# A state-space scan with a gated feed-forward block: running sums of logarithms as three bfloat16 parts, weight sums on the Vector engine in the second block, and a new order of lead-in and decays

## The chip, the cores and the metric

The kernel runs on one core of one Trainium2 chip. A core has five engines with instruction queues of their own: TensorE (PE, with its weight loads shown apart as PEld), VectorE (DVE), ScalarE (ACT), GpSimd (POOL) and SyncE (SP, which here only issues DMAs). Each queue runs in order, and engines wait for one another at semaphores. The metric is the time of one execution on the device in microseconds, as the median of several runs; less is better.

## What is computed

The reference is a chunked state-space scan (4 batches, 8 heads, 768 steps, head size 32, state size 16), followed by a normalised feed-forward block with gate (3072 tokens, 256 model columns, 1536 hidden columns). Cut to what matters:

```python
log_a = np.log(np.clip(a, 1e-6, 1.0))
for c in range(nc):                          # chunks of the sequence
    cum = np.cumsum(la, axis=-1)             # running sum of logs in the chunk
    L = np.exp(cum[..., :, None] - cum[..., None, :]) * causal
    M = np.einsum('bhin,bhjn->bhij', Cc, Bc) * L
    y[:, :, sl] = einsum(M, xc) + einsum(Cc, state) * np.exp(cum)[..., None]
    state = np.exp(la.sum(-1)) * state + einsum(Bc, xc, np.exp(cum[..., -1:] - cum))
x = y as (3072, 256)
xn = x / sqrt(mean(x * x) + 1e-6) * rms_g
g = xn @ w_gate
out = (g * sigmoid(g) * (xn @ w_val)) @ w_out
```

The three weight matrices come in as 64-bit floats, and the kernel turns them into fp32 itself.

## The kernel before

**Tiling.** The kernel uses chunks of 128 steps. Two neighbouring chunks are a pair p; two pairs (512 tokens) are a block, so there are 6 blocks and 12 pairs. The scan of block n+1 is woven into the gate products of block n. Block 0 has nothing ahead of it: its scan is the lead-in.

**Decay products.** For each pair and each half (four heads), the tile L needs the exponential of a difference of running sums, with the causal mask. `masked()` writes a large negative number above the diagonal into two PSUM banks with bfloat16 matmuls (L297). `sums()` adds the running sum of one index (L311, 128 columns each) and takes away that of the other (L316, 512 columns), as fp32 matmuls that select a row with `sel`. `decay()` is the exp on ACT (L323). The rows come from `sums_of_logs(k)`: two matmuls (L272) of the logs `la` with the running-sum matrix `mid` and its negative `nmid`, copied out by DVE and ACT (L275). That serves pairs 0 to 3. For later pairs `spread()` reads the rows back from a DRAM copy `rowd`, one row broadcast to all partitions, and `decays()` subtracts on DVE (L336), takes the exp on ACT (L339) and masks on POOL (L340).

**Rest of the scan.** `pad` and `turn` bring B and C into transposed form T (L347, L368, L370). `products` multiplies them (L391) and `decayed` applies L on DVE (L399). `scale` forms the decayed B and C (L356), `states` the states (L422 to L439), `outputs` the result y (L457, L466), which ACT evacuates as squares and as a copy (L482, L484). `norm_sums` and `norm_apply` give the normalised block xn (L494 to L513).

**Weights.** `fetch` loads a piece of a matrix, `begin` (a "b" in the plans, L156 to L165) and `finish` (an "f", L171 and L173) convert it on DVE and ACT. The plans say which step goes where, by hand.

**Gates and projection.** Block 0 uses plain products (`gate_val`, L530: tile f, 128 hidden columns; L538 is its silu, L543 the product h). Blocks 1 to 5 use a seven-product scheme for 2x2 blocks (`gates_and_values`, L582, with copies p at L587, sums c at L592, silu at L597, h at L601). It needs sums of weights, `combine_w` (L560), four operations for each of six column pairs, made on POOL during the projection of block 0, and sums of xn, `combine_x` (L567). `project` is the second product (L641), `put` copies it to `ob` on ACT (L646) and sends it out.

**What sets the order.** Nothing is scheduled by a planner: the program's text is the order on each engine. PSUM tiles rotate: `pair_of_banks` has three slots of two banks (slots 0 and 1 in a pool `first` that is closed before block 1, slot 2 in a pool that stays), `bank` two single ones. A matmul that opens a slot waits until what stood there has been read. ACT holds one function table at a time, exp or silu; `preload_act_table` loads one by hand.

Of the kernel before, what the change touches and what calls it, by code (L numbers as in the profile page):

```python
# [9 lines left out]
FP32 = mybir.dt.float32  # L10
# [9 lines left out]
def kernel(  # L20
# [208 lines left out]
    sel = const.tile([P, BH], FP32, name="sel")  # L229
    nc.vector.reduce_sum(out=sel, in_=ident.rearrange("p (c k) -> p k c", k=BH), axis=AX.X)  # L230
# [3 lines left out]
    nmid = const.tile([P, P], FP32, name="nmid")  # L234
    nc.vector.tensor_scalar(out=nmid, in0=mid, scalar1=-1.0, scalar2=None, op0=ALU.mult)
# [27 lines left out]
    nc.vector.tensor_scalar(out=la, in0=aT, scalar1=1e-6, scalar2=1.0,  # L263
                            op0=ALU.max, op1=ALU.min)
    nc.scalar.activation(out=la, in_=la, func=AF.Ln)

    rows, nrows = [], []

    def sums_of_logs(k):
        for rhs, rs, copy in ((mid, rows, nc.vector.tensor_copy), (nmid, nrows, nc.scalar.copy)):  # L270
            r_ps = bank("r_ps", (P, P))
            nc.tensor.matmul(out=r_ps, lhsT=laf[:, 2 * k * BH:(2 * k + 4) * BH], rhs=rhs,  # L272
                             start=True, stop=True)
            rs.append(const.tile([P, P], FP32, name="rows%d" % len(rows + nrows)))
            copy(out=rs[k], in_=r_ps)  # L275
# [25 lines left out]
    def sums(todo):  # L301

        work = []
        for p, half, e in todo:
            for i in range(2):
                b, c = divmod(2 * p + i, NC)
                k, q = (0, c) if c < 4 else (1, c - 2)
                work.append((slice(32 * q, 32 * q + 32), k, b * NH + 4 * half, e[:, i]))
        for o in range(4):
            for r, k, h, e in work:  # L310
                nc.tensor.matmul(out=e[:, o * P:(o + 1) * P],  # L311
                                 lhsT=sel[r, h + o:h + o + 1].to_broadcast([32, P]),
                                 rhs=rows[k][r], start=False, stop=False,
                                 tile_position=(r.start, 0), skip_group_check=True)
        for r, k, h, e in work:
            nc.tensor.matmul(out=e, lhsT=nrows[k][r],  # L316
                             rhs=sel[r, h:h + 4].unsqueeze(2).to_broadcast([32, 4, P]),
                             start=False, stop=True, tile_position=(r.start, 0),
                             skip_group_check=True)
# [234 lines left out]
    def combine_w(j, eng):  # L554
# [3 lines left out]
        for k, in0, in1, op in ((0, a21, a22, ALU.add), (1, s[:, :, 0], a11, ALU.subtract),  # L558
                                (2, a11, a21, ALU.subtract), (3, a12, s[:, :, 1], ALU.subtract)):
            eng.tensor_tensor(out=s[:, :, k], in0=in0, in1=in1, op=op)  # L560
# [8 lines left out]
    def gates_and_values(blk, todo):  # L569
# [36 lines left out]
        for j in range(last + 1):  # L606
# [37 lines left out]
    def put(blk, k, o):  # L644
        ob = ffn.tile([P, DM], FP32, tag="ob", name="ob")
# [16 lines left out]
    sums([(0, 0, ex), (1, 0, ey)])  # L662
    decay(0, 0, ex)
    decay(1, 0, ey)
    pad(0, nc.vector)
    turn(0, 0, nc.vector.tensor_copy, 3)
    turn(0, 1, nc.vector.tensor_copy, 3)
    ez = masked()
    sums([(0, 1, ez)])
    to_i, from_j = exp_of_sums()  # L670
    products(0, 0)
    decay(0, 1, ez)
    scale(0)

# [3 lines left out]
    full = const.tile([P, NC, BH], FP32, name="full")  # L678
    nc.scalar.activation(out=full, in_=full_ps, func=AF.Exp)
    pad(1, nc.gpsimd)  # L680
    turn(1, 0, nc.scalar.copy, 3)
    turn(1, 1, nc.scalar.copy, 3)
    products(0, 1)
    ew = masked()
    sums([(1, 1, ew)])
    turn_last(0, nc.scalar.copy)
    decay(1, 1, ew)
    fsel = const.tile([P, NC * NB, NH], FP32, name="fsel")
    nc.vector.tensor_tensor(
# [5 lines left out]
    products(1, 0)  # L695
    scale(1)
    outputs(0)
    products(1, 1)
    turn_last(1, nc.scalar.copy)
    states(1)  # L700
    sums_of_logs(1)
    outputs(1)
    convert("bb")
    norm_sums(0, range(NT))
    ex, ey, ez = masked(), pair_of_banks("e"), pair_of_banks("e")
    g0, g1, ew = [pair_of_banks(n) for n in ("gate", "gate", "e")]
    sums([(2, 0, ex)])
    decay(2, 0, ex)
    finish()
    finish()  # L710
    norm_apply(0, range(NT))
    products_gv(0, 0, g0)
    convert("bb")
    mask(ey)
    sums([(3, 0, ey)])
    decay(3, 0, ey)
    convert("ff")
    mask(ez)
    sums([(2, 1, ez)])
    convert("b")  # L720
    decay(2, 1, ez)
    convert("b")
# [3 lines left out]
    mask(ew)  # L726
    sums([(3, 1, ew)])
    decay(3, 1, ew)
    nc.scalar.preload_act_table(AF.Silu)
# [36 lines left out]
    todo[0] = []  # L766
    plan = ["ff", "bbf", "f", "bbf", "f", "bbf", "f", "bbf", "f", "b", "bf", ""]
    for f in range(NF):
        uv = gate_val(0, f, (g0, g1)[f] if f < 2 else None)
        convert(plan[f])  # L770
        hidden(0, f, *uv)
        if f == 3:
# [6 lines left out]
            rowd = dram.tile([NC * BH, P], FP32, name="rowd")  # L779
            nc.sync.dma_start(out=rowd[0:P], in_=rows[0])  # L780
            nc.sync.dma_start(out=rowd[P:NC * BH], in_=rows[1][2 * BH:4 * BH])
            rowv = rowd.rearrange("r m -> (r m)")
        run(todo[f])
    load_block(2)
    o = pair_of_banks("o").rearrange("p k (j m) -> p k j m", j=2)
# [76 lines left out]
```

## Time and profile before

| | us |
|---|---|
| median of 3 runs | 476.56 |
| lowest, highest | 476.41, 481.7 |
| the profiled execution | 481.5 |
| its span | 479.8 |

The span is the time from the first to the last instruction in the trace; the execution's own time is 1.7 us longer. In the profile a line such as "L641 PE MATMUL o<-wo,h ... x576 | 130.7, 386 | 4.5 <-DVE wo L173 4.5" is a group of instructions of one line and shape: how many, their busy time in us, the mean length of one in ns, then how long the engine stood idle right before them and who released it. An fp32 matmul has two records. The lengths of matmuls overlap, so the distance from one start to the next says what a matmul costs. The granted clock is that of PE: 1.00 is full speed, 0.50 is half.

### The profile page before, as it was taken

The numbers are of one execution on the slowest core, as the hardware profiler recorded it, in microseconds if no ns is written. First come the engines' busy times: TensorE is split into PE (matmuls) and PEld (weight loads), VectorE is DVE, ScalarE is ACT, GpSimd is POOL, SyncE is SP. The second block draws the span as 40 slices with busy tenths as digits, with TensorE's granted clock in tenths as the row PEclk, the third lists the DMA queues.
The fourth block names the chain that finished last, engine by engine and source line by source line (L and its number), as shares of the span: only waits on it lengthen the run. The fifth ranks groups of instructions, "written<-read, shape, count | busy, mean of one in ns | idle before, by whom it ended". The sixth has DMA issues, their size and how long they took to land.

```text
span 479.8 us, 7020 instructions
## 1 busy us (share of the span) xinstructions
PE 452.9 (94%) x2780; PEld 348.4 (73%) x2780; DVE 258.1 (54%) x486; ACT 200.3 (42%) x374; POOL 65.1 (14%) x94
## 2 busy tenths in 40 slices
PE   8989799996969999989999989999989999999997
PEld 4654344465858778878888878778878778888886
DVE  3556589759926574247555246555337551255510
ACT  3435644441545543344553254453264440145500
POOL 2020000028680000220000310001210000000000
PEclk9978899999779999999999999999999999999999
DMA  9980244582056200046200064300000000000000
GB/s 135 206 196 3 87 131 133 113 156 92 2 91 129 84 6 1 22 70 128 89 2 11 23 75 112 87 2 12 22 12 1 1 1 11 23 11 2 0 15 30
DMA packets 86656, 27.91 MB, mean 58 GB/s; under 512 B 76160, under 2 KB 80448, under 8 KB 86624
## 3 DMA queue, kind: packets, MB, share of 16 engines
q1 hardware_dynamic: 82464, 27.21, 25.0%
q10 hardware_dynamic: 4160, 0.26, 0.6%
q8 instruction: 22, 0.36, 0.3%
q14 instruction: 10, 0.08, 0.1%
HBM read 24.22 MB, written 3.24 MB: 57 GB/s over the span
## 4 chain that ended last, share of the span: by engine, by line
PE 86%; DVE 6%; ACT 4%; issue 3%; DMA 0%; POOL 0%; SPq 0%; ACTq 0%
PE gate L582 23%; PE o L641 20%; PE val L582 16%; PE gate L530 10%; PE g L391 3%; PE y L466 3%; PE tp L368 2%; PE e L311 2%; PE y L457 2%; PE e L316 1%; DVE L L336 1%; ACT p L587 1%; PE ms L494 1%; PE e L297 1%; ACT L L339 1%
## 5 line engine op out<-in xcount | busy, mean ns | idle before, releaser
L641 PE MATMUL o<-wo,h 128*128 128x256 f32 x576 | 130.7, 386 | 4.5 <-DVE wo L173 4.5
L641 PEld LDWEIGHTS o<-wo,h 128*128 128x128 f32 x576 | 110.5, 194 | 20.8 <-DVE wo L173 5.3
L592 DVE TENSOR_TENSOR c<-val,p 128x512 f32<-128x512 f32 x90 | 61.5, 691 | 84.5 <-PE val L582 54.4
L587 ACT COPY p<-gate 128x512 f32<-128x512 f32 x90 | 53.0, 589 | 48.9 <-PE gate L582 48.9
L582 PE MATMUL gate<-tx,sw 128*128 128x256 f32 x240 | 64.4, 391 | 4.9 <-ACT p L587 4.9
L582 PEld LDWEIGHTS gate<-tx,sw 128*128 128x128 f32 x240 | 43.3, 192 | 14.6 <-ACT p L587 6.3
L530 PE MATMUL gate<-xn,wgv 128*128 128x512 f32 x96 | 48.0, 646 | 4.1 <-DVE h L543 3.2
L597 ACT ACTIVATE c<-c 128x256 f32<-128x256 f32 x90 | 37.8, 420 | 32.2 <-DVE c L592 32.2
L601 DVE TENSOR_TENSOR h<-c 128x256 f32<-128x256 f32 x90 | 37.7, 419 | 13.7 <-ACT c L597 13.7
L646 ACT COPY ob<-o 128x256 f32<-128x256 f32 x24 | 8.8, 372 | 86.4 <-PE o L641 60.2
L483 POOL TENSOR_TENSOR sq<-sq 128x256 f32<-128x256 f32 x12 | 8.8, 736 | 238.5 <-ACT sq L482 238.5
L530 PEld LDWEIGHTS gate<-xn,wgv 128*128 128x128 f32 x96 | 18.7, 204 | 26.8 <-issue 20.2
L582 PE MATMUL gate<-xn,wgv 128*128 128x256 f32 x120 | 31.8, 389 | 4.0 <-ACT ob L646 4.0
L582 PE MATMUL gate<-tx,wgv 128*128 128x256 f32 x120 | 31.3, 383 | 3.4 <-ACT p L587 3.4
L582 PE MATMUL val<-xn,wgv 128*128 128x256 f32 x120 | 31.7, 387 | 0.0
L582 PE MATMUL val<-tx,sw 128*128 128x256 f32 x120 | 30.9, 380 | 0.0
L582 PE MATMUL val<-xn,sw 128*128 128x256 f32 x120 | 30.8, 379 | 0.0
L340 POOL TENSOR_SCALAR_AFFINE_SELECT L<-L 128x1024 f32<-128x1024 f32 x16 | 19.4, 1210 | 77.0 <-ACT L L339 77.0
L513 DVE SCALAR_TENSOR_TENSOR xn<-yt,gcol,rb 128x512 f32<-128x512 f32 x12 | 8.4, 746 | 39.6 <-PE rb L507 39.5
L582 PEld LDWEIGHTS gate<-xn,wgv 128*128 128x128 f32 x120 | 23.2, 194 | 7.6 <-ACT ob L646 4.4
L582 PEld LDWEIGHTS gate<-tx,wgv 128*128 128x128 f32 x120 | 22.4, 190 | 8.2 <-ACT p L587 5.4
L399 DVE TENSOR_TENSOR L<-g,L 128x1024 f32<-128x1024 f32 x16 | 19.6, 1223 | 13.0 <-PE g L391 12.4
(121 smaller groups left out, 542.1 us busy)
## 6 DMA issues: line engine op xcount, KB each, us to landing
L<-rowd SPq DMA_DIRECT2D x16, 512.0 KB, 5.6
xr<-in_x_dram SPq DMA_DIRECT2D x24, 128.0 KB, 3.6
wr<-in_moe_w_out_dram SPq DMA_DIRECT2D x6, 512.0 KB, 3.5
out_dram<-ob SPq DMA_DIRECT2D x24, 128.0 KB, 1.7
wr<-in_moe_w_gate_dram SPq DMA_DIRECT2D x5, 512.0 KB, 5.4
wr<-in_moe_w_val_dram SPq DMA_DIRECT2D x5, 512.0 KB, 4.7
br<-in_B_dram SPq DMA_DIRECT2D x22, 64.0 KB, 3.1
cr<-in_C_dram SPq DMA_DIRECT2D x22, 64.0 KB, 3.0
```

Source lines behind the costliest of these rows:

```text
L311: nc.tensor.matmul(out=e[:, o * P:(o + 1) * P], lhsT=sel[r, h + o:h + o + 1].to_broadcast([32, P]), rhs=rows[k][r], start=False, stop=Fals ...
L340: nc.gpsimd.affine_select(out=L, in_=L, pattern=[[0, NH], [1, P]], compare_op=ALU.is_ge, fill=0.0, base=0, channel_multiplier=-1)
L391: nc.tensor.matmul(out=g[:, 256 * i:256 * i + 256], lhsT=T[r, i, 0], rhs=T[r, i, 1:3].rearrange("p t m -> p (t m)"), start=(i == 0), stop= ...
L399: nc.vector.tensor_tensor(out=L, in0=g.rearrange("p q (i m) -> p q i m", i=2), in1=L, op=ALU.mult)
L466: nc.tensor.matmul(out=y[o:o + 32, h // 4, i * P:(i + 1) * P], lhsT=s["x"][:, i, h], rhs=Ls[p][:, i, h], start=opens, stop=True, tile_posi ...
L530: nc.tensor.matmul(out=gv[:, k], lhsT=w[:, t, fs], rhs=xns[blk][:, t], start=(t == 0), stop=(t == 1))
L582: nc.tensor.matmul(out=dst[:, half[w]], lhsT=lhsT, rhs=rhs[k], start=(opens and w == 0), stop=True, skip_group_check=True)
L587: nc.scalar.copy(out=t, in_=src)
L592: nc.vector.tensor_tensor(out=c, in0=b, in1=a, op=ALU.add)
L597: nc.scalar.activation(out=u, in_=c[:, half[0]], func=AF.Silu)
L601: nc.vector.tensor_tensor(out=hidden_tile(blk, j)[:, f, k], in0=u, in1=c[:, half[1]], op=ALU.mult)
L641: nc.tensor.matmul(out=o, lhsT=hs_[blk, f // 2][:, f % 2, k // 2, (k % 2) * P:(k % 2 + 1) * P], rhs=wo[:, f], start=opens, stop=(f == NF - ...
```

## The change

Five things change together.

1. **Three bfloat16 parts.** `sums_of_logs` makes rows in a new layout: partition = (chunk of four, part of four, head). One matmul with both signs (`mids`) writes 2 x 128 columns. Four DVE passes split each fp32 value: what bfloat16 keeps, what is left, what bfloat16 keeps of that, and what is left then, each on the partitions of its part. `sel` picks the three parts of a head. `sums` becomes bfloat16 matmuls, and for one chunk all five come in a row.
2. **The lead-in's order.** The second `sums_of_logs` comes right behind the first. The four mask and sums steps of pairs 2 and 3 all stand ahead of the first gate product; before, three of them stood between the gate products of f = 0, 1 and 2.
3. **Weight sums.** `combine_w` runs on DVE: two of the six late in the projection of block 0, four inside block 1. Conversions there move by one step.
4. **Decays.** The running sums for DRAM are made again in fp32 (`r_sb`, at f = 4 and 5), `tok` at f = 7, the four broadcasts start at f = 8 of the gates. In the projections of blocks 0 to 3 `decays` comes earlier, and the silu table is loaded after the second put instead of after the last.
5. **Places.** `o` of block 0 takes slot 2, `ob` gets four buffers, `fsel` moves to POOL, small tiles share memory.

```diff
     def sums_of_logs(k):
-        for rhs, rs, copy in ((mid, rows, nc.vector.tensor_copy), (nmid, nrows, nc.scalar.copy)):
...
+        nc.tensor.matmul(out=r_ps.rearrange("p s m -> p (s m)"),
+                         lhsT=la4[k].rearrange("p q k h -> p (q k h)"),
+                         rhs=mids.rearrange("p s m -> p (s m)"), start=True, stop=True)
+        first = nrm.tile([P, 2, P], BF16, tag="first", name="first", bufs=1)
+        nc.vector.tensor_copy(out=first, in_=r_ps)
+        rest = nrm.tile([P, 2, P], FP32, tag="rest", name="rest", bufs=1)
+        nc.vector.scalar_tensor_tensor(out=rest, in0=first, scalar=later_part, in1=r_ps,
+                                       op0=ALU.mult, op1=ALU.add)
+        second = nrm.tile([P, 2, P], BF16, tag="second", name="second", bufs=1)
+        nc.vector.tensor_copy(out=second, in_=rest)
+        row = const.tile([P, 2, P], BF16, name="row%d" % k)
+        nc.vector.scalar_tensor_tensor(out=row, in0=second, scalar=third_part, in1=rest,
+                                       op0=ALU.mult, op1=ALU.add)
...
     def sums(todo):
-        for o in range(4):
-            for r, k, h, e in work:
...
+                for o in range(4):
+                    nc.tensor.matmul(out=e[:, i, o * P:(o + 1) * P],
+                                     lhsT=sel[r, 4 * half + o:4 * half + o + 1].to_broadcast([32, P]),
+                                     rhs=row[r, 0], start=False, stop=False,
+                                     tile_position=(32 * q, 0), skip_group_check=True)
+                nc.tensor.matmul(out=e[:, i], lhsT=row[r, 1],
...
-            eng.tensor_tensor(out=s[:, :, k], in0=in0, in1=in1, op=op)
+            nc.vector.tensor_tensor(out=s[:, :, k], in0=in0, in1=in1, op=op)
...
             if j < last:
+                if j + 2 < last and j + 2 not in Sw:
+                    combine_w(j + 2)
...
-        ob = ffn.tile([P, DM], FP32, tag="ob", name="ob")
+        ob = ffn.tile([P, DM], FP32, tag="ob", name="ob", bufs=4)
...
     sums_of_logs(0)
-    sums([(0, 0, ex), (1, 0, ey)])
+    to_i, from_j = exp_of_sums()
+    sums_of_logs(1)
+    sums([(0, 0, ex)])
...
+    ez, ew = masked(), masked()
+    g0, g1 = pair_of_banks("gate"), pair_of_banks("gate")
+    sums([(2, 1, ez), (3, 1, ew)])
+    decay(2, 1, ez)
     products_gv(0, 0, g0)
...
-    o = pair_of_banks("o").rearrange("p k (j m) -> p k j m", j=2)
+    o = pair_of_banks("o", 2).rearrange("p k (j m) -> p k j m", j=2)
...
-        if f % 2 == 0:
-            combine_w(f // 2, nc.gpsimd)
+        if f >= 10:
+            combine_w(f - 10)
...
         for k in range(NT):
+            if blk + 2 < NBLK and k < 2:
+                decays(4 * (blk + 2) + k)
...
-            if blk + 2 < NBLK:
-                decays(4 * (blk + 2) + k)
+            if blk + 2 < NBLK and k < 2:
+                decays(4 * (blk + 2) + 2 + k)
+                if k == 1:
+                    nc.scalar.preload_act_table(AF.Silu)
```

The order on DVE at the start, before: from the clipping of `a` (written to `la`) to the first product with L.

```order
L263 TENSOR_SCALAR la<-aT 128x192
L275 COPY rows_216<-r_ps 128x128
L347 COPY cp_163<-cr 128x2x4x16
L370 COPY T<-tp 128x384 x2
L399 TENSOR_TENSOR L<-g,L 128x2x2x256
```

The same place now (`early` holds the clipped values):

```order
L276 TENSOR_SCALAR early<-aT 128x192
L306 CAST first<-r_ps 128x256
L308 SCALAR_TENSOR_TENSOR rest<-first,later_part,r_ps 128x256
L311 CAST second<-rest 128x256
L313 SCALAR_TENSOR_TENSOR row_239<-second,third_part,rest 128x256
L306 CAST first<-r_ps 128x256
L308 SCALAR_TENSOR_TENSOR rest<-first,later_part,r_ps 128x256
L311 CAST second<-rest 128x256
L313 SCALAR_TENSOR_TENSOR row_254<-second,third_part,rest 128x256
L383 COPY cp_163<-cr 128x2x4x16
L406 COPY T<-tp 128x384 x2
L435 TENSOR_TENSOR L<-g,L 128x2x2x256
```

Eight passes for the two sets of rows stand where one copy stood, and the copy into the padded C (`cp`) and the copies T are behind them.

The order on PE around the second gate tile, before: that tile's four matmuls, a mask, a sums call, the transposes of pair 2, and the gate tile f = 2.

```order
L530 MATMUL gate<-xn,wgv 128x512 x4
L297 LDWEIGHTS ident_177
L297 MATMUL e<-never_179,ident_177 128x512
L297 LDWEIGHTS ident_177
L297 MATMUL e<-never_179,ident_177 128x512
L311 MATMUL e<-rows_216,sel 128x128 x8
L316 MATMUL e<-sel,rows_220 128x512 x2
L368 MATMUL tp<-ident,br 128x128
L368 MATMUL tp<-ident,cp_163 128x128 x2
L368 MATMUL tp<-ident,Cd 128x128
L530 MATMUL gate<-xn,wgv 128x512 x4
```

The same place now, from the end of the last sums call:

```order
L348 MATMUL e<-row_254,sel 128x128
L352 LDWEIGHTS row_254
L352 MATMUL e<-sel,row_254 128x512
L566 MATMUL gate<-xn,wgv 128x512 x8
L404 MATMUL tp<-ident,br 128x128
L404 MATMUL tp<-ident,cp_163 128x128 x2
L404 MATMUL tp<-ident,Cd 128x128
L566 MATMUL gate<-xn,wgv 128x512 x4
```

The gate tiles f = 0 and 1 now follow one another, and no sums call is left between the gate tiles.

The order on ACT at the end of block 1, before: puts (`ob`), exps of the decays (L339), the silu table, and the first copies of block 2.

```order
L646 COPY ob<-o 128x256
L339 ACTIVATE L<-L 128x1024
L646 COPY ob<-o 128x256
L339 ACTIVATE L<-L 128x1024
L831 ACT_TABLE_LOAD
L587 COPY p<-gate 128x512 x2
```

The same place now:

```order
L684 COPY ob<-o 128x256
L375 ACTIVATE L<-L 128x1024
L867 ACT_TABLE_LOAD
L684 COPY ob<-o 128x256 x2
L623 COPY p<-gate 128x512 x2
```

The table load and the last exp now stand ahead of the last two puts.

More of the change, by code (lines that the diff above doesn't have):

```diff
@@ L262 @@
     laf = la.rearrange("p c h -> p (c h)")
-    nc.vector.tensor_scalar(out=la, in0=aT, scalar1=1e-6, scalar2=1.0,
+    early = nrm.tile([P, 3, NC, BH], FP32, tag="xn", name="early", bufs=1)
+    la0, full, fsel = early[:, 0], early[:, 1], early[:, 2]
+    nc.vector.tensor_scalar(out=la0, in0=aT, scalar1=1e-6, scalar2=1.0,
                             op0=ALU.max, op1=ALU.min)
-    nc.scalar.activation(out=la, in_=la, func=AF.Ln)
-    rows, nrows = [], []
-    def sums_of_logs(k):
-        for rhs, rs, copy in ((mid, rows, nc.vector.tensor_copy), (nmid, nrows, nc.scalar.copy)):
[L271 to L275, printed above, removed]
+    la4 = [const.tile([P, 4, 4, NH], FP32, name="la4%d" % k) for k in range(2)]
@@ L792 @@
             convert(plan.pop(0))
[L793 to L796 removed]
+        if f in (4, 6, 7, 9):
+            decays({4: 8, 6: 9, 7: 10, 9: 11}[f])
         if f == 0:
```

144 lines of the change are left out of this document (77 added, 67 removed).

## The prediction, written before the result was known

> **What bounds the kernel now.** I read the page first, then busy time and clock by stage, then what ended TensorE's (PE's) idle time, then single rows.
>
> ```profile
> span 479.8 us, 7020 instructions
> PE 452.9 (94%) x2780; PEld 348.4 (73%) x2780; DVE 258.1 (54%) x486; ACT 200.3 (42%) x374; POOL 65.1 (14%) x94
> PE 86%; DVE 6%; ACT 4%; issue 3%; DMA 0%; POOL 0%; SPq 0%; ACTq 0%
> ```
>
> PE is busy for 94% and carries 86% of the chain that ended last. So a saving must take work, waiting or slow clock from PE. The next view cuts the span at PE's milestones: first sums 6.81, first gate product 35.43, fourth gate tile (f = 3) 61.59, projection 103.19, block 1 137.25, block 2 207.20. Columns: stretch and its length; busy us of PE, weight load, DVE, ACT, POOL; granted clock; DMA share; GB/s. The last four rows are of PE alone: length, busy, clock.
>
> ```profile
> 6.81:35.43 28.62, 26.16 (x297) 16.65 (x297) 14.07 (x33) 11.71 (x21) 4.32 (x9) 0.90 0.94 202
> 35.43:61.59 26.16, 23.00 (x99) 10.75 (x99) 16.15 (x35) 13.54 (x20) 0.00 (x0) 0.85 0.17 50
> 61.59:103.19 41.60, 41.60 (x228) 19.59 (x227) 32.86 (x59) 19.48 (x33) 1.57 (x2) 1.00 0.50 119
> 103.19:137.25 34.06, 25.52 (x109) 21.14 (x108) 28.24 (x34) 13.21 (x19) 25.10 (x25) 0.87 0.25 75
> 137.25:207.20 69.95, 69.27 (x440) 57.57 (x441) 35.95 (x68) 29.91 (x58) 10.50 (x15) 0.96 0.26 55
> 207.20:277.20 70.00, 67.69 (x446) 56.54 (x445) 36.82 (x70) 31.27 (x60) 8.01 (x11) 1.00 0.25 54
> ...
> 29.80:39.60 9.80, 8.87 (x29) 0.50 0.52 94
> 56.94:60.30 3.36, 3.36 (x6) 0.50 0.01 2
> 118.67:125.08 6.41, 5.55 (x13) 0.50 0.01 3
> 135.70:142.11 6.41, 4.86 (x12) 0.50 0.68 114
> ```
>
> All that is lost lies before block 1, plus about 2 us in each block. Four times the clock falls to 0.50, together 26.0 us long, each time around idle PE. The groups by form name the idle time (count | busy, mean ns | idle before, releaser):
>
> ```profile
> L641 PE MATMUL o<-wo,h 128*128 128x256 f32 x576 | 130.7, 386 | 4.5 <-DVE wo L173 4.5
> L582 PE MATMUL gate<-tx,sw 128*128 128x256 f32 x240 | 64.4, 391 | 4.9 <-ACT p L587 4.9
> L530 PE MATMUL gate<-xn,wgv 128*128 128x512 f32 x96 | 48.0, 646 | 4.1 <-DVE h L543 3.2 <-DVE xn L513 0.9
> L582 PE MATMUL gate<-xn,wgv 128*128 128x256 f32 x120 | 31.8, 389 | 4.0 <-ACT ob L646 4.0
> ```
>
> **The change, part by part.** The sum is made against the profiled execution: its own time is 481.5 us, 4.9 above the median of 476.56.
>
> *Sums of logs (1: up to the first gate product).* PE rows: start, length.
>
> ```profile
> 10.02 1.16 PE L311 MATMUL e<-rows,sel 32*128 32x128 f32 x16
> 11.01 1.03 PE L316 MATMUL e<-sel,rows 32*128 32x512 f32 x4
> 11.97 0.59 PE L281 MATMUL d_ps<-la,upto 128*128 128x192 f32 x2
> ...
> 43.60 0.61 PE L297 MATMUL e<-never,ident 128*128 128x512 bf16 x2
> 44.14 1.16 PE L311 MATMUL e<-rows,sel 32*128 32x128 f32 x16
> 46.09 3.70 PE L530 MATMUL gate<-xn,wgv 128*128 128x512 f32 x8
> ...
> 6.47 0.29 DVE L275 COPY rows<-r_ps 128x128 f32<-128x128 f32 x1 [1.30 <-PE r_ps L272]
> ```
>
> One fp32 call of sums() for half a pair holds PE from 10.02 to 11.97: 1.95 us for 2048 columns, with two row groups side by side. In bfloat16 two 512-column matmuls take 0.54 us (43.60 to 44.14), so 2048 columns need 1.06. That is the low end. The high end is no gain, 1.95: the new loop keeps five matmuls in one row group, so weight loads may show and the pairs no longer run side by side. I take 1.4, the middle nearer to the bfloat16 row, since the columns are the larger part.
>
> The Trainium skill, "TensorE: Matmul & The Clock Gate", Part 3, says that a weight load overlaps a running matmul only when the row group differs. By that rule most of the ten loads of a call are exposed, the call costs about 1.9 and the sum below is 4 us longer. No row here has bfloat16 loads repeated in one row group; the fp32 rows above, which alternate, cannot decide it.
>
> On DVE one 0.29 us copy (6.47) becomes four dependent passes over 256 columns, 0.42 each by the Cd row in the next view: the first sums start 1.4 us later. The second chain of four (1.7) stands ahead of the pad and the T copies on DVE, so PE's transposes wait for it; one sums call (1.4) covers all but 0.3. Eight calls at 1.4 and three more masks at 0.54 make 12.8 us of PE before the first gate product; before, four calls of 1.95 and one at half clock (3.7), two of them merged, made 9.6. Together 1.4 + 0.3 + 3.2 = +4.9. Against it: the calls of pairs 2 and 3 now fill PE where the norm was waited for (0.9 of the L530 row, and about 1 us around the norm sums), and if PE stays busy the half clock from 29.80 to 35.43 goes, 2.5 us of its 5.6. ACT's logarithm becomes four, of which only the first stands ahead of the first sums, and POOL, 4.32 us busy of 28.62, gets the two copies of `mids` and the product `fsel`: nothing. Net **+0.5** (ends -3: no weight load shows; +3: the half clock stays).
>
> *New order of the gates (2: first gate to f = 3).* Three mask and sums stretches of 2.49 us (43.60 to 46.09) leave it: 7.5. The wait for `h` (3.2) goes, because g0 and g1 now run when the remaining exps are already queued, and both half-clock stretches (4.2 and 3.4 us, all busy) halve: 3.8. Together 14.5; what is late next is the conversion of the weights for f = 2, 0.1. **-14.4** (ends -15.5, -10).
>
> *Rest of the gates (3).* DVE, 55 to 100 us:
>
> ```profile
> L543 DVE TENSOR_TENSOR h<-u,gate 128x512 f32<-128x512 f32 x11 | 7.5, 683 | 5.6 <-ACT u L538 5.5
> L165 DVE SCALAR_TENSOR_TENSOR m<-wr,m 128x512 f32<-128x512 uint32 x10 | 7.3, 733 | 0.3
> L171 DVE SCALAR_TENSOR_TENSOR e<-wr,e 128x512 int32<-128x512 int32 x9 | 6.2, 687 | 4.2 <-ACT e L160 4.2
> L173 DVE SCALAR_TENSOR_TENSOR wgv<-m,e 128x512 f32<-128x512 f32 x8 | 5.5, 692 | 0.3
> L399 DVE TENSOR_TENSOR L<-g,L 128x1024 f32<-128x1024 f32 x4 | 4.9, 1219 | 0.0
> L156 DVE TENSOR_SCALAR e<-wr 128x512 int32<-128x512 int32 x10 | 4.2, 420 | 0.0
> L356 DVE TENSOR_TENSOR Cd<-cr,d_sb 128x256 f32<-128x256 f32 x1 | 0.4, 418 | 0.0
> ```
>
> A begin is 2 x 0.42 + 0.73 = 1.57 us, a finish 1.38. From the norm to the last gate DVE has 12 begins, 11 finishes, 11 products h, 4 decays of 1.22 and about 7 us of small work: 18.8 + 15.2 + 7.5 + 4.9 + 7 = 53.4. PE needs about 11.8 + 41.6 from the first gate. PE has caught up with DVE, so DVE's waits for ACT (4.2 us here) begin to show: +1.6. Two small matmuls for the rows sent to DRAM: +0.9. **+2.5** (ends +0.9, +5). Their two DMAs and the four broadcasts stand behind the weight fetches on SP, some 10 us before their first use: nothing.
>
> *Projection of block 0 (4).* POOL 106 to 140, DVE 103 to 134, PE:
>
> ```profile
> L560 POOL TENSOR_TENSOR sw<-wgv 128x256 f32<-128x256 f32 x12 | 11.7, 977 | 0.0
> L340 POOL TENSOR_SCALAR_AFFINE_SELECT L<-L 128x1024 f32<-128x1024 f32 x4 | 5.5, 1368 | 5.6 <-ACT L L339 5.6
> ...
> L165 DVE SCALAR_TENSOR_TENSOR m<-wr,m 128x512 f32<-128x512 uint32 x4 | 4.0, 990 | 0.1
> L156 DVE TENSOR_SCALAR e<-wr 128x512 int32<-128x512 int32 x4 | 2.2, 554 | 0.0
> ...
> 105.73 3.70 PE L641 MATMUL o<-wo,h 128*128 128x256 f32 x16
> 109.27 0.60 PE L507 MATMUL rb<-ident,rs 128*128 128x128 f32 x4
> ```
>
> While POOL combines weights (24 operations near 0.97), DVE's same forms slow from 0.42 to 0.55 and from 0.73 to 0.99, and PE waits 4.5 us for `wo`, then 4.0 for `ob`, each followed by half clock. With POOL's 23 us gone, PE alone needs 96 records at 3.54 / 16 (105.73 to 109.27), 21.2, and 1.6 of norm: 22.8. DVE needs 0.7 + 4 x 1.57 + 5 x 1.38 + 1.4 + 1.7 + 4 x 1.22 = 21.9 before its eight combinations (3.4); its last `wo` ends near 21, and 16 records (3.5) follow: 24.5. The four affine selects stay on POOL: +1. The tile `o` moves to a slot outside the pool that closes, so the 4.0 goes. 34.06 becomes 25.5: **-8.5** (ends -11.3; -4 if all four selects of 1.37 hold DVE up).
>
> *Block 1 (5).* PE's 4.86 us at half clock from 137.25 halve: -2.4. DVE gets 16 combinations of 0.42, 6.7 us, onto 35.95 of 69.95. Ahead of a sum that PE waits for they cost between 0 and 6.7; I take 1.5, near the low end as DVE is half idle. **-0.9**.
>
> *Ends of blocks 1 to 3 (6).*
>
> ```profile
> 209.78 1.28 ACT L831 ACT_TABLE_LOAD   x1
> ...
> 211.07 0.59 ACT L587 COPY p<-gate 128x512 f32<-128x512 f32 x1
> ...
> 211.71 1.13 PE L582 MATMUL gate<-tx,sw 128*128 128x256 f32 x4 [1.63 <-ACT p L587]
> ```
>
> The last exp and the table load stand ahead of the copy `p`; PE waits 1.63. In the new order the load comes two puts earlier, under projections of about 5 us each. 3 x 1.63: **-4.9** (other end 0). More `ob` buffers: 0, no steady block waits for one.
>
> Sum: +0.5 - 14.4 + 2.5 - 8.5 - 0.9 - 4.9 = -25.7. From the profiled 481.5: 455.8. The median run is already 4.9 faster; what it lacks I cannot see. If it lacks part of the same waits and half clock, 455.8 stands; if not, 450.9. I take **453.5**.
>
> **The rivals.**
> *DVE becomes the bound.* Combinations, splits and conversions share one in-order queue. For: 53.4 us of DVE against about the same of PE in the gates. Against: 51% busy in block 1. If block 1 pays 6.7, the gates +5 and the projection -4: 5.2 + 2.5 + 4.5 longer, 465.7.
> *The conversions do not speed up*, because something else than POOL slows them; the 4.5 wait and its half clock (5.55 busy, 2.8 lost) stay: 460.8. Against: uncontended rows of the same forms before 100 us.
> *Slower: the clock.* Half clock from the first sums to f = 3, where short matmuls and waits mix, as from 29.80 to 39.60. PE has some 40 us of work there; all at half would add about 35: 488. It decides only beyond 32 us. Against: 6.81 to 29.80 holds the same kinds of matmul, and the stage's mean of 0.90 with 5.6 us at 0.50 at its end leaves 1.00 for them.
>
> **How the numbers follow.** Forecast near 453.5 (446 to 461): 0.70. DVE as bound: 0.16. Conversions not faster: 0.06. More saved than forecast, below 446: 0.06. Slower: 0.02. The range, 444 to 466, leaves out some 1 in 10 and holds every rival but the slow clock. A measurement of this kernel can tell about 2%, that is 467.0 and 486.1: faster 0.92, within 2% 0.06, slower 0.02.
>
> **What would show it.** First gate product near 36, f = 3 near 48, projection near 92, block 1 near 117; a sums call of 1.1 to 1.9; no wait for `h`, `wo` or `ob` over 1 us; clock 1.00 from 40 on; DVE forms at 0.42 and 0.73 throughout; no 1.63 at block ends. Wrong if PE waits for DVE in the gates or block 1, or if the clock still halves.

## The result and the profile after

| | before | after |
|---|---|---|
| median, us | 479.13 (4 runs) | 452.38 (4 runs) |
| lowest, highest | 476.41, 481.91 | 451.95, 452.72 |
| the profiled execution | 481.5 | 452.72 |

The ratio is 0.944, with a 95% interval of 0.937 to 0.952: faster by 5.6%. The forecast was 453.5. The executions of the kernel before read either near 476.5, with a mean granted clock of 0.982, or near 481.7, with 0.972, so a median moves with the mix, and below lengths of stages and mean clocks stand beside medians.

The page of the changed kernel begins so; the third line is the chain that ended last, by engine.

```profile
span 450.6 us, 6872 instructions
PE 433.6 (96%) x2700; PEld 336.9 (75%) x2700; DVE 264.7 (59%) x521; ACT 199.9 (44%) x375; POOL 48.4 (11%) x73
PE 82%; DVE 9%; SPq 4%; DMA 2%; ACT 2%; issue 1%; POOL 0%; DVEq 0%
```

PE's busy time fell by 19.3 us (452.9 to 433.6) and the span by 29.2; the other 10 us were time in which PE was idle. DVE's share of the chain rose from 6% to 9%. The next view cuts the span as the one of before did (first sums, first gate product, f = 3, projection, block 1, block 2, block 3, and last the only stretch at half clock); its columns are the same.

```profile
8.19:32.02 23.83, 21.33 (x275) 13.22 (x274) 15.84 (x36) 11.76 (x20) 4.27 (x8) 0.93 0.90 205
32.02:44.55 12.53, 11.52 (x34) 5.45 (x34) 12.03 (x29) 10.50 (x16) 0.63 (x2) 1.00 0.48 129
44.55:89.10 44.55, 42.28 (x233) 19.86 (x231) 37.12 (x68) 21.90 (x37) 1.46 (x2) 1.00 0.52 152
89.10:114.25 25.15, 22.95 (x108) 19.37 (x109) 23.51 (x38) 11.65 (x14) 5.77 (x5) 1.00 0.29 36
114.25:184.01 69.76, 68.21 (x446) 56.65 (x444) 44.39 (x88) 32.98 (x64) 11.39 (x16) 1.00 0.27 60
184.01:252.39 68.38, 67.70 (x445) 56.49 (x444) 37.09 (x69) 31.34 (x60) 9.18 (x11) 1.00 0.26 55
11.84:15.25 3.41, 3.41 (x21) 1.88 (x21) 1.89 (x3) 1.57 (x3) 0.00 (x0) 0.50 0.89 255
```

The large gains stand where they were forecast: 26.16 to 12.53 between the first gate product and f = 3, 34.06 to 25.15 in the projection. Of 27.3 us at half clock (10.24, 3.41, 6.83 and 6.83; the prediction's windows hold 26.0 of them), 3.41 are left. The view of what PE waited for, summed over the span (us, times, longest), names what remains:

```profile
PE gate L618 <- ACT p L623: 4.0, 6, 0.7
PE o L679 <- DVE wo L173: 2.2, 3, 1.0
PE o L679 <- DVE h L579: 1.4, 1, 1.4
...
PE gate L566 <- DVE wgv L173: 1.0, 1, 1.0
PE tp L404 <- DVE cp L383: 0.9, 1, 0.9
```

The waits of 4.0 (`ob`) and 3.2 (`h`, ahead of f = 2) of before are gone, and the 4.5 for `wo` are 2.2 in three pieces. New are 1.4 for another `h`, the last one, 1.0 for `wgv` and 0.9 for `cp`.

### The profile page after: what moved, and what is told of

The parts are those of the page before. It is cut to its first block, busy times and chain, and to the rows that moved or that the text cites. A ratio compares the mean times of both kernels' runs of the same rounds, so it can differ in the third digit from the quotient of the medians.

```text
span 450.6 us, 6872 instructions
## 1 busy us (share of the span) xinstructions
PE 433.6 (96%) x2700; PEld 336.9 (75%) x2700; DVE 264.7 (59%) x521; ACT 199.9 (44%) x375; POOL 48.4 (11%) x73
## 4 chain that ended last, share of the span: by engine, by line
PE 82%; DVE 9%; SPq 4%; DMA 2%; ACT 2%; issue 1%; POOL 0%; DVEq 0%
PE o L679 24%; PE gate L618 24%; PE val L618 17%; PE gate L566 6%; PE g L427 3%; PE y L502 2%; PE tp L404 2%; DMA wr<-in_moe_w_gate_dram 2%; DVE e L171 1%; PE y L493 1%; SPq L108 1%; DVE L L372 1%; SPq L146 1%; DVE m L165 1%; SPq L114 1%; DVE wgv L173 1%
## 5 line engine op out<-in xcount | busy, mean ns | idle before, releaser
L679 PE MATMUL o<-wo,h 128*128 128x256 f32 x576 | 128.3, 380 | 3.6 <-DVE wo L173 2.2
L679 PEld LDWEIGHTS o<-wo,h 128*128 128x128 f32 x576 | 108.3, 190 | 19.8 <-DVE wo L173 3.4
L566 PE MATMUL gate<-xn,wgv 128*128 128x512 f32 x96 | 43.6, 598 | 1.0 <-DVE wgv L173 1.0
L566 PEld LDWEIGHTS gate<-xn,wgv 128*128 128x128 f32 x96 | 17.4, 190 | 20.1 <-issue 17.4
L618 PE MATMUL gate<-xn,wgv 128*128 128x256 f32 x120 | 30.8, 379 | 0.0
L618 PEld LDWEIGHTS val<-tx,sw 128*128 128x128 f32 x120 | 22.5, 190 | 4.1 <-DVE c L628 1.2
```

The lines of the kernel that those rows point to most:

```text
L566: nc.tensor.matmul(out=gv[:, k], lhsT=w[:, t, fs], rhs=xns[blk][:, t], start=(t == 0), stop=(t == 1))
L618: nc.tensor.matmul(out=dst[:, half[w]], lhsT=lhsT, rhs=rhs[k], start=(opens and w == 0), stop=True, skip_group_check=True)
L679: nc.tensor.matmul(out=o, lhsT=hs_[blk, f // 2][:, f % 2, k // 2, (k % 2) * P:(k % 2 + 1) * P], rhs=wo[:, f], start=opens, stop=(f == NF - ...
```

## The experiments

Each kernel is the changed one with the edit shown. A time that is compared with nothing else is compared with the changed kernel's 452.38. Lengths of stages and rows come from the profiled executions.

### What the sums cost

**All sums in one row group.** Three of four chunks then read another chunk's rows. A row group here is the set of 32 PE rows that one chunk's sums use (32*128 in the rows below).

```diff
-                q = 2 * (p % 2) + i
-                r, row = slice(32 * q, 32 * q + 32), rows[p // 2]
+                q = 0
+                r, row = slice(0, 32), rows[p // 2]
```

> The changed kernel, with all sums matmuls on the rows of the first chunk of a set, so that every one of them sits in the first row group of PE (the rows of the other chunks are not used). Theory (a sums call takes 0.6 us because the two chunks' matmuls, in different row groups, run side by side although each chunk's five stand in a row): a call takes 1.0 to 1.4 us, the four calls before the first gate product cost 2 to 3 us more, the time is 454 to 456. Rival (bfloat16 matmuls of 32 rows are that cheap one after the other): a call stays at 0.6 and the time within 0.5 of 452.4.

**Fp32 sums.** The split, the second and third part, and the bfloat16 type go; the order stays.

```diff
-        first = nrm.tile([P, 2, P], BF16, tag="first", name="first", bufs=1)
...
-        row = const.tile([P, 2, P], BF16, name="row%d" % k)
...
+        row = const.tile([P, 2, P], FP32, name="row%d" % k)
+        nc.vector.tensor_copy(out=row, in_=r_ps)
```

> Fp32 rows and an fp32 selector in place of the three bfloat16 parts: one DVE pass a set instead of four, the sums as fp32 matmuls, five in a row for a chunk as in the changed kernel. Theory: a call of 2048 columns takes about 1.95 us as in the kernel before, instead of 0.60; eight calls are 10.8 longer, less about 3.0 for the six passes left out: 458 to 462, first gate product near 40. If five fp32 matmuls in one row group expose their weight loads, a call takes 2.3 or more. Rival: part of the longer calls fills PE where it waited for rs and T (1.6 us) and the time is 455 to 458.

**One part alone.** As the last, but rows and selector stay bfloat16, so the decays lose precision. It leaves out the second and third part of the running sums.

> The changed kernel with rows as one bfloat16 part: the second and third part are left out, and with them three DVE passes for each of the two sets. Theory (the split delays the lead-in): the first sums start 1.2 us earlier, PE's wait of 0.9 us for the padded C goes, the half clock of 12 to 15 us may go with it, and the time is 449 to 451. Rival (the split is hidden, because the conversions of the weights set the end of the lead-in): 452.4 within 0.5.

The first sums call on PE and the instruction behind it, in the changed kernel:

```profile
8.19 0.40 PE L348 MATMUL e<-row,sel 32*128 32x128 bf16 x7
8.41 0.37 PE L352 MATMUL e<-sel,row 32*128 32x512 bf16 x1
8.43 0.21 PE L348 MATMUL e<-row,sel 32*128 32x128 bf16 x1
8.49 0.37 PE L352 MATMUL e<-sel,row 32*128 32x512 bf16 x1
8.79 0.33 PE L404 MATMUL tp<-ident,br 128*128 128x128 f32 x1
```

in one row group:

```profile
8.20 0.38 PE L349 MATMUL e<-row,sel 32*128 32x128 bf16 x4
8.41 0.37 PE L353 MATMUL e<-sel,row 32*128 32x512 bf16 x1
8.63 0.38 PE L349 MATMUL e<-row,sel 32*128 32x128 bf16 x4
8.85 0.37 PE L353 MATMUL e<-sel,row 32*128 32x512 bf16 x1
9.16 0.33 PE L405 MATMUL tp<-ident,br 128*128 128x128 f32 x1
```

in fp32, and then, in the view by stretch, the part of its lead-in at half clock:

```profile
7.88 1.26 PE L340 MATMUL e<-row,sel 32*128 32x128 f32 x10
...
9.65 1.02 PE L344 MATMUL e<-sel,row 32*128 32x512 f32 x2
10.60 0.33 PE L396 MATMUL tp<-ident,br 128*128 128x128 f32 x1
```

```profile
36.48:53.55 17.07, 17.07 (x61) 10.49 (x58) 8.02 (x21) 7.65 (x11) 1.18 (x4) 0.50 0.01 1
```

From the first start to the next instruction, 2048 columns take 0.60 us in the changed kernel, 0.96 in one row group, and 2.72 in fp32 in this order. In the changed kernel the matmuls of the two chunks, in different row groups, lie over one another: the second 512-column matmul starts 0.08 after the first, in one row group 0.44 after it. The last call of the lead-in, for pairs 2 and 3 and so with all four row groups, takes only 0.77 for 4096 columns (31.25 to 32.02).

The kernel in one row group read 455.21, 456.48 and 457.44 at mean clocks of 0.989 to 0.996, and 464.87 to 465.04 three times at 0.966 to 0.971; the profiled execution, 464.87, was at half clock for 20.5 us from 11.66 and for 10.2 from 38.97. The reading at the changed kernel's usual clock, 0.996, is 2.5 above the changed kernel's slowest; eight calls by 0.36 are 2.9, near the expected 2 to 3 us (all eight stand before the first gate product, not four). The call itself, 0.96, is just under the expected 1.0 to 1.4. The median, 461.15, is set by the clock. With fp32 sums: 469.83, above the 458 to 462 expected. The call was dearer than in the kernel before (2.72, not 1.95), which is at most 17.0 for eight, since the g products already start under some of them, and 17.1 us at half clock came on top. The projection starts at 106.44 instead of 89.10; from there on nothing differs. One part alone: 449.38, 3.0 less, as expected, with the projection at 85.83. The first sums start 0.68 earlier, not 1.2; the wait for `cp` and the half clock are gone. So the passes that are left out are on the path.

### The second split and the pad

**Second split later**, behind the first `scale`:

```diff
-    sums_of_logs(1)
     sums([(0, 0, ex)])
...
     scale(0)
+    sums_of_logs(1)
     products(1, 0)
```

> The changed kernel with the second set of rows, which only pairs 2 and 3 need, made later: its matmul and its four DVE passes stand behind the scaling of pair 0, where DVE idles. Theory (the second split holds the padded C and the T copies up): PE's wait of 0.9 us at 10 us goes and with it perhaps the half clock that follows it, and the time is 449.5 to 451.5. Rival (what is gained is waited for at the next place, the conversion of the weights for f = 2): 452.4 within 0.5.

**Pad first:**

```diff
+    pad(0, nc.vector)
     sums_of_logs(1)
     sums([(0, 0, ex)])
     decay(0, 0, ex)
-    pad(0, nc.vector)
```

> The copy of C into its padded form moves ahead of the second split on DVE; all else as in the changed kernel. Theory: the wait of 0.89 for cp at 10.13 goes, and the 3.1 us of half clock that follow it with it; PE needs the second rows only at 18.6. Expected 449.9 to 451.5 (0.9 for the wait, up to 1.5 for the clock), first gate product near 30.5. Rival: what PE does not wait for here it waits for at the T copies or at the norm a few us later, 452.4 plus or minus 0.4.

The transposes behind the first sums call on PE, with the idle time before in brackets: first the changed kernel, then the one with the pad first, and of that also the stretch that had run at half clock:

```profile
8.96 0.27 PE L404 MATMUL tp<-ident,cp 128*128 128x128 f32 x1
10.13 0.33 PE L404 MATMUL tp<-ident,cp 128*128 128x128 f32 x1 [0.89 <-DVE cp L383]
```

```profile
8.97 0.38 PE L404 MATMUL tp<-ident,cp 128*128 128x128 f32 x2
```

```profile
11.84:15.25 3.41, 3.41 (x30) 2.40 (x31) 2.56 (x4) 2.10 (x4) 0.00 (x0) 1.00 0.93 263
```

Pad first: 450.87 (450.48 to 451.64), 1.5 below the changed kernel, as expected. The wait is gone, those 3.41 us hold 30 matmul records instead of 21, the first gate product comes at 29.96 instead of 32.02, and the 2.0 stay to the end of the span (448.6). At a mean clock of 1.000 in both, 450.48 and 450.67 stand against 452.06, so some 1.5 are the wait and what follows from it, not the clock. One part alone, 449.25 to 449.42 at the same clock, is only 1.2 below that: more than half of the split's price lies in the place where it stands.

That the wait also causes the half clock behind it is not shown. The kernel with `o` in a rotating slot, further down, has the same lead-in and the same wait, and PE runs at full clock from 12.00 to 15.10; its half clock comes at 29.92:

```profile
10.62 0.33 PE L404 MATMUL tp<-ident,cp 128*128 128x128 f32 x1 [0.90 <-DVE cp L383]
```

Second split later: 451.70, a gain of 0.7 and less than expected. Here PE's idle time moved ahead of the first sums (1.23 us, released by the first split's last pass on DVE, L313), and 3.41 us at half clock turned up later, from 28.24.

### The lead-in's order

**Sums of pairs 2 and 3 among the gate tiles again**, in bfloat16, in the order of the kernel before. The exps, the conversions and the silu table load that stood around them move back with them:

```diff
     sums([(2, 0, ex)])
-    norm_sums(0, range(NT))
+    decay(2, 0, ex)
+    finish()
+    finish()
+    norm_apply(0, range(NT))
+    products_gv(0, 0, g0)
+    convert("bb")
+    mask(ey)
     sums([(3, 0, ey)])
...
+    mask(ez)
+    sums([(2, 1, ez)])
+    convert("b")
     decay(2, 1, ez)
...
     products_gv(0, 1, g1)
...
+    mask(ew)
+    sums([(3, 1, ew)])
+    decay(3, 1, ew)
+    nc.scalar.preload_act_table(AF.Silu)
```

> The changed kernel with one part undone: three of the four mask and sums steps of pairs 2 and 3 stand between the gate tiles f = 0, 1 and 2 again, with the bfloat16 sums kept. Theory (the order, and not the cheaper sums, took away the wait for h and the half clock there): the steps cost the same in either place, PE waits again for h before f = 2, 2 to 4 us, with some half clock after it, and the time is 455 to 459. Rival (the cheap sums did it): within 1 us of 452.4.

459.89, so 7.5 slower and just above the 455 to 459 expected; the projection starts at 96.16, 7.1 later, and all stages behind it are as long as in the changed kernel. Rows of PE:

```profile
26.64 0.61 PE L530 MATMUL ms<-mean,sq 128*128 128x1 f32 x4 [1.05 <-POOL sq L519]
31.07 5.15 PE L566 MATMUL gate<-xn,wgv 128*128 128x512 f32 x8 [0.93 <-DVE xn L549]
38.38 3.70 PE L566 MATMUL gate<-xn,wgv 128*128 128x512 f32 x8
46.86 5.40 PE L566 MATMUL gate<-xn,wgv 128*128 128x512 f32 x8 [3.15 <-DVE h L579]
```

All three waits of the kernel before are back with nearly their old sizes (1.1, 0.9, 3.2), and so is half clock: eight records of a gate tile take 5.15 and 5.40 around them, 3.70 between. Half clock lasts 6.83 us from 27.23 and 3.41 from 47.71. With fp32 sums in the new order, the other way round, PE waits for no `h` before f = 2. So the order, not the type of the sums, removes the wait for `h`; which of the steps that moved together does it was not tried apart.

### The projection of block 0

**Sums of weights on POOL again**, every second step:

```diff
...
-        if f >= 10:
-            combine_w(f - 10)
+        if f % 2 == 0:
+            combine_w(f // 2, nc.gpsimd)
```

> The changed kernel with one part undone: the sums of weights are made on POOL again, four operations at every second step of block 0's projection. Theory (POOL operations that read SBUF hold DVE's passes up, and the conversions of wo come late): the 512-wide passes of begin go from 0.69 to about 0.99 us in the projection, PE waits at least 4 us for wo in one piece and runs at half clock after it, the projection takes 31 to 34 us instead of 25.2, the time is 458 to 462. Rival (the conversions were slow for another reason, and the order of begin and finish cured it): the passes stay near 0.69 and the time within 1 us of 452.4.

461.50, 462.00 and 463.60 at mean clocks near 0.99, and 468.53 at 0.971. The middle one of the first three is 9.6 slower, at the upper end of the 458 to 462 expected. The projection takes 28.97 (90.67 to 119.64) instead of 25.15, less than the 31 to 34 expected, and the wait for `wo` is 6.0 in three pieces, not one, with no half clock behind it. Rows of PE, then groups of DVE (95 to 125 us) and POOL (95 to 130), with count | busy, mean ns:

```profile
104.94 3.72 PE L679 MATMUL o<-wo,h 128*128 128x256 f32 x16 [2.31 <-DVE wo L173]
110.11 3.72 PE L679 MATMUL o<-wo,h 128*128 128x256 f32 x16 [1.45 <-DVE wo L173]
116.08 3.72 PE L679 MATMUL o<-wo,h 128*128 128x256 f32 x16 [2.25 <-DVE wo L173]
128.28 0.71 PE L404 MATMUL tp<-ident,cp 128*128 128x128 f32 x2 [4.28 <-POOL cp L383]
```

```profile
L171 DVE SCALAR_TENSOR_TENSOR e<-wr,e 128x512 int32<-128x512 int32 x4 | 4.7, 1176 | 0.0
L173 DVE SCALAR_TENSOR_TENSOR wo<-m,e 128x512 f32<-128x512 f32 x4 | 4.3, 1086 | 0.1
...
L596 POOL TENSOR_TENSOR sw<-wgv 128x256 f32<-128x256 f32 x12 | 11.4, 948 | 0.0
```

Beside POOL's work DVE's L171 takes 1.18 us on average instead of 0.86 in the changed kernel's projection, and L173 1.09 instead of 0.85. These are passes of finish. The passes of begin, of which the theory spoke, stayed at 0.42 and 0.69; POOL made no sum and no select when they started. The larger part of the loss lies later: the pad of pair 4 on POOL stands behind the sums of weights and the selects, PE waits 4.28 for it, 3.41 us at half clock follow, and block 1 is 75.29 long instead of 69.76. Another 1.6 us come in the lead-in, with a second stretch of half clock.

**No affine selects** on the four decays of this projection. It leaves out their causal mask.

```diff
...
-            decays({4: 8, 6: 9, 7: 10, 9: 11}[f])
+            decays({4: 8, 6: 9, 7: 10, 9: 11}[f], False)
```

> The changed kernel without the causal masking on POOL of the four decays in block 0's projection (that masking is left out). Theory (each of POOL's selects over SBUF holds one DVE pass up for its own length): DVE's finish passes there go from 0.86 to 0.69 us, PE's waits for wo of 1.0 and 0.65 us shrink to under 0.5 in all, and the time is 450 to 451.3. Rival (PE waits because DVE simply has more work than PE there): 452.4 within 0.5.

449.50 to 450.54 in three of four executions, 1.8 to 2.9 below the changed kernel's median (450 to 451.3 was expected). The fourth, 460.48, is the profiled one; it was at half clock for 27.3 us of its first 42. Its projection runs at full clock:

```profile
11.14:35.03 23.89, 23.63 (x194) 13.43 (x192) 10.02 (x22) 7.50 (x14) 2.05 (x3) 0.50 0.88 208
99.08:122.60 23.52, 22.84 (x109) 19.38 (x110) 21.94 (x40) 12.46 (x14) 2.69 (x5) 1.00 0.30 37
```

It takes 23.52, and PE waits 0.54 for `wo`, once. That the slow lead-in does not shorten it shows in the kernel with one row group, which keeps the selects: there 30.7 us at half clock go ahead, and the projection takes 25.16. DVE's finish passes take 0.70 and 0.69, as expected. What the selects do to DVE shows in the changed kernel, POOL and DVE by start:

```profile
103.81 1.19 POOL L376 TENSOR_SCALAR_AFFINE_SELECT L<-L 128x1024 f32<-128x1024 f32 x1 [10.53 <-ACT L L375]
103.97 1.58 DVE L171 SCALAR_TENSOR_TENSOR e<-wr,e 128x512 int32<-128x512 int32 x1
...
108.47 0.68 DVE L171 SCALAR_TENSOR_TENSOR e<-wr,e 128x512 int32<-128x512 int32 x1
108.57 3.02 POOL L376 TENSOR_SCALAR_AFFINE_SELECT L<-L 128x1024 f32<-128x1024 f32 x2 [3.56 <-ACT L L375]
109.18 1.46 DVE L173 SCALAR_TENSOR_TENSOR wo<-m,e 128x512 f32<-128x512 f32 x1
```

A pass that starts before a select keeps its 0.68; one that starts under it ends about 0.55 after the select does: L171 at 105.55 after a select that ends at 105.00, L173 at 110.64 after the first of the two, 1.53 long, that ends at 110.10.

**Late decays**: as pad first, and all four decays behind the last conversion.

```diff
...
-        if f in (4, 6, 7, 9):
-            decays({4: 8, 6: 9, 7: 10, 9: 11}[f])
...
+        if f == 8:
+            for g in range(8, 12):
+                decays(g)
```

> As the run with the early pad, and the four decays of the projection of block 0 stand behind the last conversion of wo. Theory: the affine selects on POOL held the last conversions (1.58 and 1.46 us passes instead of 0.68), and the subtractions of 1.2 us stood ahead of them, so without both the waits for wo fall from 2.2 to about 1 us; the projection is near 24 instead of 25.15, and the time 0.8 to 1.5 below the run with the early pad. Rival: the decays only move the wait to the weight sums and to the copy p of block 1, no gain or up to 1 us slower.

452.23, 1.4 above pad first: no gain, as the rival had it, and more than the 1 us slower that it allowed. The projection fell to 22.94 with one wait of 0.52 for `wo`, but block 1 grew from 69.76 to 72.96. Rows of DVE, POOL and PE:

```profile
106.90 6.54 POOL L376 TENSOR_SCALAR_AFFINE_SELECT L<-L 128x1024 f32<-128x1024 f32 x4 [14.58 <-ACT L L375]
109.96 1.30 DVE L596 TENSOR_TENSOR sw<-wgv 128x256 f32<-128x256 f32 x1
114.19 1.13 PE L618 MATMUL gate<-tx,sw 128*128 128x256 f32 x4 [1.23 <-ACT p L623]
116.44 2.00 PE L618 MATMUL val<-tx,sw 128*128 128x256 f32 x4 [1.13 <-DVE c L628]
```

The selects, now in one piece, hold the sums of weights (1.30 instead of 0.42), and two waits of over 1 us follow, with 3.41 us at half clock from 116.55. The same profile also has 3.41 us at half clock from 27.80. The one execution at a mean clock of 1.000 took 451.0, against 450.48 and 450.67 of pad first.

**`o` in a rotating slot**, as before:

```diff
-    o = pair_of_banks("o", 2).rearrange("p k (j m) -> p k j m", j=2)
+    o = pair_of_banks("o").rearrange("p k (j m) -> p k j m", j=2)
```

> The changed kernel with one part undone: block 0's output tile o takes the next slot in turn, in the pool that is closed before block 1. Theory (the place of o alone took away most of the old 4.0 us wait): block 1's first matmul waits for the four copies of o, 1.5 to 2.5 us, and the time is 453.5 to 455. Rival (the four buffers of ob and the earlier exps took it away): no wait over 0.5 us there, 452.4 within 0.5.

452.81, no difference that can be told, and below the 453.5 to 455 expected. The wait for `ob` is there, as expected, but another one goes. PE in the kernel with the rotating slot, then in the changed one:

```profile
87.11 1.89 PE L679 MATMUL o<-wo,h 128*128 128x256 f32 x8
...
114.47 1.34 PE L618 MATMUL gate<-xn,wgv 128*128 128x256 f32 x4 [1.91 <-ACT ob L684]
```

```profile
89.10 1.99 PE L679 MATMUL o<-wo,h 128*128 128x256 f32 x8 [1.41 <-DVE h L579]
```

In slot 2 `o` starts 1.41 us late, waiting for the last product `h` on DVE; in the rotating slot it does not wait there. That fits a gate tile that stood in slot 2 and had to be read first, which was not tested. A placement free of both waits was not tried.

### Block ends and the state order

**Old order of decays and silu table** in blocks 1 to 3:

```diff
-            if blk + 2 < NBLK and k < 2:
-                decays(4 * (blk + 2) + k)
...
-            if blk + 2 < NBLK and k < 2:
-                decays(4 * (blk + 2) + 2 + k)
-                if k == 1:
-                    nc.scalar.preload_act_table(AF.Silu)
+            if blk + 2 < NBLK:
+                decays(4 * (blk + 2) + k)
...
+        if blk + 2 < NBLK:
+            nc.scalar.preload_act_table(AF.Silu)
```

> The changed kernel with one part undone: in blocks 1 to 3 each decay stands behind its put again, and the silu table is loaded after the last one. Theory: PE waits 1.6 us for the copy p at the start of blocks 2, 3 and 4, 4.9 in all: 457.3, between 456.8 and 457.8. Rival (other changes freed ACT there, so that the order no longer matters): 452.4 within 0.5.

456.63, 4.25 slower and just under the 456.8 to 457.8 expected. Blocks 2, 3 and 4 are 69.99, 69.87 and 70.25 long instead of 68.38, 68.28 and 68.65, 4.8 together, and the wait of before is back at each start; PE at the second of them, block 3:

```profile
257.53 1.13 PE L618 MATMUL gate<-tx,sw 128*128 128x256 f32 x4 [1.59 <-ACT p L623]
```

**State order**: as late decays, with the last transposes and states of pair 1 ahead of the outputs of pair 0.

```diff
-    outputs(0)
     turn_last(1, nc.scalar.copy)
     states(1)
+    outputs(0)
     outputs(1)
```

> As the run with the late decays, and the last transposes and the states of pair 1 stand ahead of the outputs of pair 0. Theory: ACT's T copy no longer stands behind two evacuations of y, so PE's wait of 0.74 goes: 0.4 to 0.8 below the run with the late decays. Rival: the outputs of pair 0 come later, so its squares come later and the norm takes the wait: no gain.

451.96 (450.23 to 452.64) against 452.23 (451.0 to 452.59): undecided. The wait of 0.74 for the copy T is gone, but the first gate product, 30.99, came no earlier than in the profile of late decays (30.93); both have 3.41 us at half clock just ahead of it.

## Why the prediction was right, and where its terms were off

Profile against profile 25.7 was predicted and 28.8 measured (481.5 to 452.72). By the terms:

1. **Sums of logs: +0.5 predicted, -3.4 measured** (first gate product at 32.02, not 36). This is the mis-sized term, and the step is "I take 1.4, the middle nearer to the bfloat16 row" for a call of 2048 columns: it is 0.60, below even the low end of 1.06. That end came from 512-column matmuls that follow one another; here the two row groups of a call lie over one another, although each chunk's five matmuls stand in a row. In one row group the call takes 0.96. Eight calls by 0.8 are 6.4 us; the forecast was missed by 3.9, so some 2.5 were lost again, to the wait for `cp`, the half clock at 11.84 and the 0.74 for T. The rule from the Trainium skill ("TensorE: Matmul & The Clock Gate", Part 3), that a weight load overlaps a running matmul only when the row group differs, did not decide here: with every load in one row group the call takes 0.96 and not 1.9, and four loads of its second five (8.42 to 8.84) run beside the 512-column matmul of its first (from 8.41, 0.37 long). For fp32 the order may matter: 2.72 with five in a row, 1.95 with groups alternating. The same Part says that tiles in different row groups run side by side; the 0.08 us between the two 512-column matmuls agrees.
The split's price was right for the first chain (first sums at 8.19, 1.4 later) and too small for the second: "one sums call (1.4) covers all but 0.3". With a call of 0.60 the cover was gone, and PE waits 0.89. Putting the pad ahead of the split returns 1.5 us.
2. **Order of the gates: -14.4, measured -13.6.** Putting the order back lengthens this stage by 8.9 (31.07 to 52.53) and brings the wait for `h` and half clock back. The rest is not undone there: the sums stay cheap. What came late next was the conversion for f = 2, as said, but 1.01 and not 0.1.
3. **Rest of the gates: +2.5, measured +2.95.** The waits for DVE's `h` (0.86 at 53.92, 1.41 at the end) carry most. The second is not DVE's lateness but the slot of `o`, a cost that the prediction did not name, so that the size fits is in part luck.
4. **Projection: -8.5, measured -8.9** (25.15; 25.5 predicted). POOL's sums of weights were the cause of part of it: with them back the projection is 3.8 longer. The selects cost 1.6 there, where 1 was put. The reason given for `o` was wrong in effect: moving it removes a wait of 1.91 at the end and sets one of 1.41 at the start. What took the rest of the old 4.0 away was not tried.
5. **Block 1: -0.9, measured -1.2.** The prediction's milestone of 207.20 is not the start of block 2: its first gate product comes at 208.19, so block 1 was 70.94 long before, not 69.95, and is 69.76 now. DVE is busy 44.39 of it; PE's longest wait in it is 0.67, for the copy `p`.
6. **Ends of blocks: -4.9, measured -4.9.** Confirmed by undoing it.

The rivals: DVE did not become the bound; the conversions sped up except under a select; the clock fell for 3.41 us only. Two of the signs of being wrong came up all the same, small: PE waits for DVE in the gates (1.01 and 0.86), and the clock halves once. Nor is the clock safe with short matmuls. With fp32 sums or one row group the profiled lead-ins spent 17.1 and 30.7 us at half clock, and the run without selects, whose lead-in is the changed kernel's own, spent 27.3; that execution took 10.8 longer than the middle one of the other three. A loss of 10.8 is below the 32 at which this rival would have decided, and the changed kernel's own four executions show none of that size.

That 453.5 came within 1.1 of the median is in part luck. It took the median as halfway between two readings; against the profiled run the terms summed to 455.8, 3.1 too high, which is mostly term 1, and the 2.3 taken off made up for it. What the faster readings of before lack is half clock: the mean clocks differ by 0.010, which over some 477 us is an estimated 4.8 us, the distance of the two groups.

The best version is the changed kernel with the pad first: 450.87. The two kernels below it leave out parts of the sums or masks.

## What to carry to other kernels

Price a group of small matmuls by the distance from its start to the next instruction, with the row groups as they will be, not by the lengths of single rows. Undo each part alone before saying which one paid: fp32 sums cost 17.4 us, the sums of weights on POOL 9.6, the old order of the lead-in 7.5, the old order at the ends of blocks 4.2, the old slot of `o` nothing. Together that is more than the whole gain, since waits or half clock come back with each, and since fp32 sums are dearer in the new loop than in the old one. When a tile gets a fixed place, look up who read that place last, since a wait at the end can become one at the start.

## What was not expected of the hardware

- Half clock comes in stretches of 3.41 us (changed kernel, from 11.84) and of whole multiples: 6.83 and 10.24 (before), 17.07 (fp32 sums), 20.48 (one row group), 23.89 (no selects). The Trainium skill ("TensorE: Matmul & The Clock Gate", Part 1) states a free-running window of 3413 ns. The lengths agree. No idle gap of that length is needed: with fp32 sums PE waits nowhere longer than 0.74 us between 7 and 36 us, and half clock starts at 36.48. A short gap does not decide it either: the wait of 0.89 at 10.13 has half clock behind it in the changed kernel, the same wait in the kernel with the rotating slot has not. Five kernels here share one lead-in (changed, sums on POOL, rotating slot, old decays, no selects), and their profiled executions spend 3.4, 6.8, 3.4, 3.4 and 27.3 us of the first 45 at half clock. What sets it stays open.
- A select of 1.2 to 1.5 us on POOL holds a conversion pass on DVE that starts under it (L171, 0.68 to 1.58; L173, 0.69 to 1.46), while one that starts just before it is not held.
